# Retention attention feeding a top-1 mixture of experts: the attention stages of a block put in order of TensorE's tile shape

## The chip, the cores and the metric

One core of one Trainium2 chip runs the whole program. The metric is device time in microseconds (us), the median of a few runs. The core has five engines that run side by side and meet at semaphores: TensorE (PE, with its weight loads shown as PEld), VectorE (DVE), ScalarE (ACT), GpSimd (POOL) and SyncE (SP), and 16 DMA engines that move data.

## The reference

For 8 batches, 8 heads, 576 tokens and head size 64, attention is linear with a decay per head; its output goes through one of eight experts per token.

```python
scores = scale * np.matmul(q, k.transpose(0, 1, 3, 2))
gamma = 1.0 - 2.0 ** (-5.0 - np.arange(H))
Dmat = np.where(rel >= 0, gamma[:, None, None] ** rel, 0.0)   # rel = row - column
attn = np.matmul(scores * Dmat, v)                            # [B, H, S, 64]
x = attn.transpose(0, 2, 1, 3).reshape(B * S, H * 64)         # 4608 x 512
logits = x @ w_gate                                           # 8 experts
expert_idx, gate_w = argmax(logits), softmax(logits) at the argmax
for e in range(8):
    out[mask_e] = gate_w[mask_e] * (relu(x[mask_e] @ w1[e]) @ w2[e])   # 512 -> 1024 -> 512
```

## The kernel before

The program has two phases. The first computes the attention, writes its rows in bf16 to a DRAM tensor `x_rows`, and computes the gate's logits and the routing of the first half of the tokens beside it. The second gathers each expert's rows, multiplies them with that expert's weights and scatters the results. Only the first phase is touched by the change.

**Blocks.** A batch is cut into five blocks: c = 0 to 3 have 128 tokens, c = 4 has the remaining 64. There are 40 blocks, and block i is (b, c) = (i // 5, i % 5). The decay is split into a factor on q and one on k, so the masked scores need only a 0/1 mask, and a running state (sum of k times v, kept in the PSUM tile `pss`) carries what earlier blocks contribute. The stages of a block, and the shapes in which they use TensorE's 128 by 128 array:

- `scale_q` and `scale_k` (L241 to L256) run on POOL and multiply q and k by their factors, giving `qq` and `kk`.
- `stage_TQ` and `stage_TK` (L258, L268) transpose `qq` and `kk` on PE (full array, 128 by 128) into a PSUM buffer of the pool `psw`, which has three buffers; ACT copies the result to `qT` (L266) and `kT` (L276). `stage_TQ(b + 1, c)` prepares a quarter of the next batch's q in each of the blocks c = 0 to 3.
- `stage_S` (L279) adds k times v to `pss` (128 by 64) and ACT copies the state to `se` (L293).
- `stage_SC` (L296) computes scores into `pssc` (64 by 64), and DVE multiplies them with the mask into `sc` (L311, L324 for a remainder block).
- `stage_AV` (L331) multiplies scores with values (128 by 64; 64 by 64 in a remainder block) and then the state with q (64 by 64), both into `psx`; DVE copies `psx` to `xT` (L351). In a remainder block ACT first copies half of it (`xo`, L370) and DVE adds the two (`xTr`, L372).
- `stage_R` transposes `xT` back (full array, tile `psr`), ACT casts it to `xr`, and SP stores it to `x_rows`.
- `stage_L1` and `stage_L2`, once a batch, compute the logits (128 by 32, tile `psl`), and transpose them into `lg`.

**Order.** The order on each engine is written out by hand: each engine executes its instructions in the order in which the Python code emits them, and waits at each for its semaphores. The loop `for i, (b, c) in enumerate(blocks)` emits one iteration per block, in a software pipeline: iteration i holds the scores of block i+1, the k transposes of block i+2, the state of block i+1, the transposes back of block i-1, and the value and state products of block i. The scaling runs ahead: iteration i emits `scale_q(b + 1, c)` and `scale_k(i + 3)`.

**Loads.** `load_k(i + 6)`, `load_v(i + 6)` and `load_q(b + 2, ...)` are issued on SP, and the experts' first weights (`load_w`, L224) on POOL, whose DMA casts them to bf16. To pace them, each waits for a mark: a recent instruction named "sc" (the masking), "kT" (the copy of transposed k) or "xT" (the copy of psx), taken as it stands where the load is emitted. One weight load is emitted at the end of iterations 12, 16, 20, 24 and 28, and three at the end of each of the last seven iterations:

```python
early = {12 + 4 * j: [(0, j)] for j in range(5)}
for i in range(NB - 7, NB):
    early[i] = [rest.pop(0) for _ in range(3)]
...
for (e, j), m in zip(early.get(i, ()), ("sc", "kT", "xT")):
    load_w(e, j, 4, wpool, mark.get(m))
```

**Routing.** `route_first` is a Python generator started in block (4, 1), i = 21. It yields an estimated DVE cost after each small instruction, and `steps(rf, budget)` emits instructions until the budget is spent; a `yield None` ends a call at once. Such a break stands ahead of the ranks (PE tile `psrk`, and DVE's `ntot`, `ova`, `rk`, `pos`), ahead of the placing (`pspl`), and ahead of each of the four calls of `gather(e, 0)`, each of which emits two indirect DMAs on POOL.

Of the kernel before, what the change touches and what calls it, by code (L numbers as in the profile page):

```python
# [20 lines left out]
B, H, S, DH = 8, 8, 576, 64  # L21
DM = H * DH
E, F = 8, 1024
NP = H // 2
NCH = 4
# [16 lines left out]
def kernel(  # L42
# [236 lines left out]
    def stage_S(i):  # L279

        if i >= NB:
            return
        b, c = blocks[i]
        kk = kks.pop(i)
        if c == NCH:
            return
        for p in range(NP):
            for j in range(2):
                h = 2 * p + j
                mm(pss[j * DH:(j + 1) * DH, p * DH:(p + 1) * DH], kk[:, h, :], vts[i][:, h, :],  # L290
                   c == 0 and p == 0, c == NCH - 1)
        se = wkp.tile([P, NP, DH], F32, tag="se")
        mark["se"] = nc.scalar.copy(out=se[:, :, :].rearrange("p a d -> p (a d)"), in_=pss[:, 0:NP * DH])  # L293
        sts[(b, c + 1)] = se

    def stage_SC(i):  # L296
        if i >= NB:
            return
        b, c = blocks[i]
        kT = kTs.pop(i)  # L300
        sc = wkp.tile([P, 2, NP, P], F32, tag="sc")
        scs[i] = sc
        if c < NCH:
            qT = qTs[b]
            for p in range(NP):
                for u in range(2):
                    for j in range(2):
                        r = slice(j * DH, (j + 1) * DH)
                        mm(pssc[u * DH:(u + 1) * DH, j, p * P + u * DH:(p + 1) * P], kT[r, p, u * DH:(u + 1) * DH],
                           qT[r, p, c * P + u * DH:(c + 1) * P], True, True)  # L310
            mark["sc"] = nc.vector.tensor_tensor(  # L311
                out=sc[:, :, :, :].rearrange("p j a i -> p j (a i)"), in0=pssc[:, :, :],
                in1=mask[:, :, :].rearrange("p a i -> p (a i)").unsqueeze(1).to_broadcast([P, 2, NP * P]),
                op=ALU.mult)
        else:
            qTs[(b, "r")] = kT
            for p2 in range(2):
                for hf in range(2):
                    p = 2 * hf + p2
                    for j in range(2):  # L320
                        r = slice(j * DH, (j + 1) * DH)
                        mm(pssc[hf * DH:(hf + 1) * DH, j, p2 * P + DH:(p2 + 1) * P], kT[r, p, DH:P], kT[r, p, 0:DH],
                           True, True)
            mark["sc"] = nc.vector.tensor_tensor(  # L324
                out=sc[:, :, 0:2, 0:DH],
                in0=pssc[:, :, :].rearrange("p j (a u i) -> p j a u i", u=2, i=DH)[:, :, 0:2, 1, :],
                in1=tri[:, :].unsqueeze(1).unsqueeze(1).to_broadcast([P, 2, 2, DH]), op=ALU.mult)
# [2 lines left out]

    def stage_AV(i):  # L331
        b, c = blocks[i]
        vt = vts.pop(i)
        sc = scs.pop(i)
        if c < NCH:
            for p in range(NP):
                for j in range(2):
                    o = (j ^ (p % 2)) * DH
                    mm(psx[o:o + DH, j, (p // 2) * P:(p // 2 + 1) * P], vt[:, 2 * p + j, :], sc[:, j, p, :],
                       p < 2, c == 0 and p >= 2)  # L340
            if c > 0:
                se, qT = sts.pop((b, c)), qTs[b]
                for p in range(NP):
                    for j in range(2):
                        o = (j ^ (p % 2)) * DH
                        r = slice(j * DH, (j + 1) * DH)
                        mm(psx[o:o + DH, j, (p // 2) * P:(p // 2 + 1) * P], se[r, p, :], qT[r, p, c * P:(c + 1) * P],
                           False, p >= 2)
            if c == 0:
                xTs[b] = wk1.tile([P, NCH, NP * P], F32, tag="xT", name="xT")  # L350
            mark["xT"] = nc.vector.tensor_copy(  # L351
                out=xTs[b][:, c, :].rearrange("p (w t) -> p w t", w=2), in_=psx[:, :, 0:2 * P])
        else:
            se, qT = sts.pop((b, c)), qTs.pop((b, "r"))
            x = psx[:, :, 256:512].rearrange("p w (a u t) -> p w a u t", a=2, u=2)
            for p2 in range(2):
                for hf in range(2):
                    r = slice(hf * DH, (hf + 1) * DH)
                    for j in range(2):
                        o = (j ^ p2) * DH  # L360
                        mm(x[o:o + DH, hf, p2, hf, :], vt[r, 2 * p2 + j, :], sc[r, j, p2, 0:DH], p2 == 0, False)
            for hf in range(2):
                for p2 in range(2):
                    for j in range(2):
                        r = slice(j * DH, (j + 1) * DH)
                        o = (j ^ p2) * DH
                        mm(x[o:o + DH, j, p2, hf, :], se[r, 2 * hf + p2, :], qT[r, 2 * hf + p2, 0:DH],
                           False, hf == 1 and p2 == 1)
            xo = wk1.tile([P, 256], F32, tag="xo", name="xo")
            nc.scalar.copy(out=xo[:, :], in_=psx[:, 1, 256:512])  # L370
            xTs[(b, "r")] = wk1.tile([P, 256], F32, tag="xTr", name="xTr")
            mark["xT"] = nc.vector.tensor_tensor(out=xTs[(b, "r")][:, :], in0=psx[:, 0, 256:512], in1=xo[:, :],  # L372
                                                 op=ALU.add)
# [70 lines left out]
    def make_routing():  # L444

        nc.gpsimd.memset(lg[:, :, :], 0.0)
        nc.gpsimd.memset(su1[:, :], -1.0)
        nc.gpsimd.affine_select(out=su1[:, :], in_=su1[:, :], pattern=[[-1, P]], base=0, channel_multiplier=1,
                                compare_op=ALU.is_ge, fill=0.0)
        nc.gpsimd.memset(onesb[:, :], 1.0)  # L450
        nc.gpsimd.tensor_copy(out=identb[:, :], in_=ident[:, :])
        nc.gpsimd.iota(iota_r[:, :], pattern=[[1, P]], base=0, channel_multiplier=0,
                       allow_small_or_imprecise_dtypes=True)
        nc.gpsimd.iota(rev[:, :], pattern=[[-1, E]], base=E, channel_multiplier=0,
                       allow_small_or_imprecise_dtypes=True)
        nc.gpsimd.memset(off[:, :], 0.0)
        nc.gpsimd.memset(off[REM:P, :].rearrange("p (b c) -> p b c", c=NCOL)[:, :, NCH:NCOL], 100.0)
        nc.gpsimd.memset(rst[:, :, :], 1.0)
        nc.gpsimd.memset(rst[:, :, 0:1], 0.0)
        nc.gpsimd.iota(hi[:, :], pattern=[[S // 64, B], [2, NCOL]], base=0, channel_multiplier=0,  # L460
                       allow_small_or_imprecise_dtypes=True)
        nc.gpsimd.iota(lo[:, :], pattern=[[1, 1]], base=1, channel_multiplier=1,
                       allow_small_or_imprecise_dtypes=True)
        nc.gpsimd.tensor_copy(out=fld[:, :, 0], in_=hi[:, :])
        nc.gpsimd.tensor_copy(out=fld[:, :, 1], in_=lo[:, :].to_broadcast([P, NT]))
# [170 lines left out]
    def steps(g, budget):  # L636

        while budget > 0:
            try:
                c = next(g)  # L640
            except StopIteration:
                return False
            if c is None:
                break
            budget -= c
        return True
# [38 lines left out]
    rf = None  # L685
    for i, (b, c) in enumerate(blocks):
        if i == 1:
            make_routing()
        if c < NP and b + 1 < B:
            scale_q(b + 1, c)  # L690
        scale_k(i + 3)
        stage_SC(i + 1)
        load_k(i + 6, mark.get("sc"))
        stage_TK(i + 2)
        stage_S(i + 1)
        if c in (1, 3) and b + 2 < B:
            load_q(b + 2, c // 2, mark.get("kT"))
        if rf is not None:
            steps(rf, 0.6)
        if i > 0:  # L700
            stage_R(i - 1)
        if c == 0 and b > 0:
            stage_L1(b - 1)
        stage_AV(i)
        load_v(i + 6, mark.get("xT"))
        if c < NP and b + 1 < B:
            stage_TQ(b + 1, c)
        if c == 0 and b > 0:
            stage_L2(b - 1)
        for (e, j), m in zip(early.get(i, ()), ("sc", "kT", "xT")):  # L710
            load_w(e, j, 4, wpool, mark.get(m))
        if (b, c) == (B // 2, 1):
            rf = route_first()
        if rf is not None:
            steps(rf, 0.8)
    for e, j in rest:
        load_w(e, j, 4, wpool)
    while steps(rf, 1.0):
# [229 lines left out]
```

## Time and profile before

| what | value |
|---|---|
| median of 3 runs | 382.88 us (382.41 to 383.18) |
| the profiled execution's own time | 384.02 us |
| span of its profile | 382.2 us, so 1.8 us lie outside it |
| busy share of PE, PEld, DVE, ACT, POOL | 90%, 64%, 43%, 34%, 52% |
| attention loop, expert phase | until about 207 us, from 212 us |
| one batch of attention in the steady part | 22.57 us |
| DMA, mean | 171 GB/s |

The profile is of one execution. A row of the timeline gives the start and the length in us, the engine, the source line, the operation, the output and input tiles, and the number of instructions merged; in brackets stands the engine's idle time before the row, and what ended it. For PE the array shape that a matmul uses (rows * columns) and the size of the moving operand follow. An fp32 matmul shows as several passes. Matmul ends are modelled, so starts are the better measure. The granted clock is the share of full speed that TensorE was given.

### The profile page before, as it was taken

The page shows a single profiled execution, that of the slowest core. Times are in us where ns is not written, and L with a number is a line of the kernel's source. Part 1 is how long each engine was busy: PE and PEld are TensorE (multiplying, and loading weights), DVE is VectorE, ACT ScalarE, POOL GpSimd, SP SyncE. Part 2 cuts the span into 40 slices and gives each one's busy share as a digit, 9 for nine tenths or more (in the row PEclk, how much of TensorE's full clock was granted, in tenths as well). Part 3 has the DMA queues.
Part 4 walks back from the last instruction along what each step waited for, and adds up shares of the span by engine and source line. Part 5 has one row for each costly group of instructions (what it writes and reads, how often), then busy time and mean ns, then how long its engine had stood idle before and what let it go on. Part 6 is the DMA issues. An engine that isn't in the chain of part 4 may idle for free.

```text
span 382.2 us, 11126 instructions
## 1 busy us (share of the span) xinstructions
PE 342.5 (90%) x4642; PEld 243.2 (64%) x4642; DVE 165.3 (43%) x358; ACT 130.3 (34%) x292; POOL 197.4 (52%) x241
## 2 busy tenths in 40 slices
PE   2599999999999979999994799899999999999960
PEld 1477877778778767877773567555556565656520
DVE  3043343434445786847971695322233232323220
ACT  2224535254353433524331222244322323242410
POOL 4875343453625253587646247867566555554230
PEclk9769999999999999999999699999999999999995
DMA  8958877788888677997999999799789222323120
GB/s 208 250 99 195 204 189 185 168 209 208 206 205 207 162 175 186 180 218 183 196 216 222 207 220 206 199 209 203 178 203 206 93 98 95 103 98 107 63 72 9
DMA packets 113083, 65.34 MB, mean 171 GB/s; under 512 B 83838, under 2 KB 105342, under 8 KB 113024
## 3 DMA queue, kind: packets, MB, share of 16 engines
q0 software_dynamic: 18176, 31.47, 37.3%
q1 hardware_dynamic: 93792, 32.02, 35.1%
q10 hardware_dynamic: 1056, 1.05, 0.9%
q8 instruction: 39, 0.64, 0.7%
q14 instruction: 20, 0.16, 0.2%
HBM read 67.14 MB, written 15.20 MB: 215 GB/s over the span
## 4 chain that ended last, share of the span: by engine, by line
PE 84%; DVE 5%; DMA 4%; POOL 2%; issue 1%; ACT 1%; POOLq 0%; DVEq 0%
PE pm L60 19%; PE py L60 18%; PE psx L60 13%; PE pssc L60 9%; PE psk L63 6%; PE pss L60 5%; PE psr L63 5%; PE psq L63 4%; DMA w1b<-in_moe_w_dram 2%; PE pt L63 2%; PE psl L60 1%; DMA kt<-in_k_dram 1%; DVE xt L757 1%; DVE pay L576 1%; PE pspl L60 1%
## 5 line engine op out<-in xcount | busy, mean ns | idle before, releaser
L773 ACT ACTIVATE ht<-pm 128x384 bf16<-128x384 f32 (+1 forms) x96 | 50.5, 527 | 100.9 <-PE pm L60 100.3
L60 PE MATMUL pm<-xt,w1b 128*128 128x256 bf16 (+1 forms) x512 | 74.5, 305 | 5.4 <-DMA w1b<-in_moe_w_dram 4.9
L788 POOL DMA_INDIRECT out_dram<-ys,tids x40 | 40.9, 1021 | 59.9 <-DVE ys L787 53.2
L60 PE MATMUL py<-w2b,ht 128*128 128x512 bf16 x320 | 71.7, 379 | 0.0
L60 PEld LDWEIGHTS <-w1b 128*128 128x128 bf16 x512 | 51.0, 100 | 28.3 <-DMA w1b<-in_moe_w_dram 5.0
L254 POOL TENSOR_TENSOR kk<-kt,kg 128x512 f32<-128x512 f32 x40 | 41.9, 1056 | 41.0 <-PE pss L60 31.5
L60 PEld LDWEIGHTS <-ht 128*128 128x128 bf16 x320 | 30.7, 98 | 34.1
L311 DVE TENSOR_TENSOR sc<-pssc,mask 128x1024 f32<-128x1024 f32 x32 | 39.1, 1221 | 29.0 <-PE pssc L60 15.3
L787 DVE TENSOR_SCALAR ys<-py,gat 128x512 f32<-128x512 f32 x40 | 30.0, 750 | 47.5 <-PE py L60 46.2
L630 POOL DMA_INDIRECT xg<-x_rows,tidg x40 | 41.1, 1027 | 12.4 <-issue 7.5
L244 POOL TENSOR_TENSOR qq<-qt,qg 128x512 f32<-128x512 f32 x32 | 34.3, 1073 | 19.4 <-PE psq L63 10.3
L351 DVE COPY xT<-psx 128x512 f32<-128x512 f32 x32 | 22.1, 691 | 47.7 <-PE psx L60 47.7
L276 ACT COPY kT<-psk 128x512 f32<-128x512 f32 x40 | 23.4, 586 | 48.8 <-PE psk L63 48.0
L60 PE MATMUL psx<-sc,vt 128*64 128x128 f32 (+1 forms) x640 | 39.2, 270 | 0.0
L757 DVE COPY xt<-pt 128x512 bf16<-128x512 bf16 x40 | 15.5, 420 | 52.6 <-PE pt L63 47.3
L63 PE MATMUL psk<-ident,kk 128*128 128x128 f32 x160 | 27.6, 298 | 11.4 <-POOL kk L254 11.4
L60 PE MATMUL pssc<-qT,kT 64*64 64x64 f32 (+1 forms) x1024 | 37.0, 262 | 0.5 <-ACT se L293 0.5
L60 PEld LDWEIGHTS psx<-sc,vt 128*64 128x64 f32 (+1 forms) x640 | 30.2, 137 | 6.0 <-issue 4.9
L60 PEld LDWEIGHTS pssc<-qT,kT 64*64 64x64 f32 x1024 | 28.7, 137 | 5.7 <-issue 3.1
L232 POOL DMA_DIRECT2D w1b<-in_moe_w_dram x24 | 15.2, 639 | 27.8 <-DVE sc L311 14.9
L266 ACT COPY qT<-psq 128x512 f32<-128x512 f32 x32 | 19.2, 599 | 28.8 <-PE psq L63 28.7
L63 PEld LDWEIGHTS psk<-ident,kk 128*128 128x128 f32 x160 | 17.6, 146 | 17.5 <-POOL kk L254 11.6
(118 smaller groups left out, 350.2 us busy)
## 6 DMA issues: line engine op xcount, KB each, us to landing
kt<-in_k_dram SPq DMA_DIRECT2D x32, 256.0 KB, 4.7
vt<-in_v_dram SPq DMA_DIRECT2D x32, 256.0 KB, 4.3
qt<-in_q_dram SPq DMA_DIRECT2D x14, 512.0 KB, 5.8
x_rows<-xr SPq DMA_DIRECT2D x32, 128.0 KB, 5.4
w1b<-in_moe_w_dram POOLq DMA_DIRECT2D x16, 256.0 KB, 6.9
w2b<-in_moe_w_dram POOLq DMA_DIRECT2D x16, 256.0 KB, 7.6
w1b<-in_moe_w_dram POOLq DMA_DIRECT2D x8, 512.0 KB, 9.6
w2b<-in_moe_w_dram POOLq DMA_DIRECT2D x8, 512.0 KB, 7.6
```

What stands on the lines that cost most here:

```text
L60: nc.tensor.matmul(out=out, lhsT=lhsT, rhs=rhs, start=start, stop=stop, skip_group_check=True)
L63: nc.tensor.transpose(out=out, in_=in_, identity=identity)
L244: nc.gpsimd.tensor_tensor(out=qq[:, :, :].rearrange("p s (h d) -> p h s d", d=DH), in0=qts[b][:, h0:h0 + 2, :, :], in1=qg[:, 0:NCH, h0:h0 ...
L254: nc.gpsimd.tensor_tensor(out=kk[:, :, :], in0=kts.pop(i)[:, :, :], in1=kg[:, blocks[i][1], :].unsqueeze(2).to_broadcast([P, H, DH]), op=A ...
L276: mark["kT"] = nc.scalar.copy(out=kT[:, :, :].rearrange("p a t -> p (a t)"), in_=pst[:, :])
L311: mark["sc"] = nc.vector.tensor_tensor(out=sc[:, :, :, :].rearrange("p j a i -> p j (a i)"), in0=pssc[:, :, :], in1=mask[:, :, :].rearrang ...
L351: mark["xT"] = nc.vector.tensor_copy(out=xTs[b][:, c, :].rearrange("p (w t) -> p w t", w=2), in_=psx[:, :, 0:2 * P])
L630: nc.gpsimd.indirect_dma_start(out=xg[:, :], out_offset=None, in_=x_rows[0:nr, :], in_offset=bass.IndirectOffsetOnAxis(ap=slots[ph][1][:, ...
L757: nc.vector.tensor_copy(out=xt[:, :, j * P:(j + 1) * P], in_=pt[:, :, :])
L773: nc.scalar.activation(out=ht[:, f0:f0 + per, :], in_=pm[:, :, :], func=AF.Relu)
L787: nc.vector.tensor_scalar(out=ys[:, :], in0=py[:, :], scalar1=gat[:, i:i + 1], scalar2=None, op0=ALU.mult)
L788: nc.gpsimd.indirect_dma_start(out=next(outs)[:, :], out_offset=bass.IndirectOffsetOnAxis(ap=tids[:, i:i + 1], axis=0), in_=ys[:, :], in_o ...
```

## The change

The iteration of the block loop is put in another order, so that all stages that use one array shape stand together. The state-times-q part of `stage_AV`, with the copy of `psx`, becomes a stage of its own, `stage_IN`; in a remainder block it also holds the value products. An iteration now runs: k and q transposes, the transposes of the logits (`stage_L2`, one block later than before, at c = 1), the transposes back, the logits, then `stage_S` and `stage_AV`, then `stage_IN` and the scores of block i+1. The two calls of the routing generator become one at the end, with the sum of their budgets. `load_k` is still ahead of the k transposes, so its mark "sc" is now the masking of block i instead of i+1; the weight loads are still at the end of the iteration.

```diff
     def stage_AV(i):
         b, c = blocks[i]
-        vt = vts.pop(i)
-        sc = scs.pop(i)
         if c < NCH:
+            vt = vts.pop(i)
+            sc = scs.pop(i)
             for p in range(NP):
...
+
+    def stage_IN(i):
+
+        b, c = blocks[i]
+        if c < NCH:
             if c > 0:
                 se, qT = sts.pop((b, c)), qTs[b]
...
         else:
+            vt = vts.pop(i)
+            sc = scs.pop(i)
             se, qT = sts.pop((b, c)), qTs.pop((b, "r"))
...
         if c < NP and b + 1 < B:
             scale_q(b + 1, c)
         scale_k(i + 3)
-        stage_SC(i + 1)
         load_k(i + 6, mark.get("sc"))
         stage_TK(i + 2)
-        stage_S(i + 1)
+        if c < NP and b + 1 < B:
+            stage_TQ(b + 1, c)
+        if c == 1 and b > 0:
+            stage_L2(b - 1)
+        if i > 0:
+            stage_R(i - 1)
         if c in (1, 3) and b + 2 < B:
             load_q(b + 2, c // 2, mark.get("kT"))
-        if rf is not None:
-            steps(rf, 0.6)
-        if i > 0:
-            stage_R(i - 1)
         if c == 0 and b > 0:
             stage_L1(b - 1)
+        stage_S(i + 1)
         stage_AV(i)
+        stage_IN(i)
+        stage_SC(i + 1)
         load_v(i + 6, mark.get("xT"))
-        if c < NP and b + 1 < B:
-            stage_TQ(b + 1, c)
-        if c == 0 and b > 0:
-            stage_L2(b - 1)
         for (e, j), m in zip(early.get(i, ()), ("sc", "kT", "xT")):
             load_w(e, j, 4, wpool, mark.get(m))
         if (b, c) == (B // 2, 1):
             rf = route_first()
         if rf is not None:
-            steps(rf, 0.8)
+            steps(rf, 1.4)
```

## The prediction, made before the changed kernel ran

> **What bounds the kernel now.** First the chain of waits on the page: it runs through TensorE (PE) for most of the span.
>
> ```profile
> PE 84%; DVE 5%; DMA 4%; POOL 2%; issue 1%; ACT 1%; POOLq 0%; DVEq 0%
> ```
>
> Then busy time by stretches of one batch of attention (columns: stretch in us, its length, then busy us and instructions of PE, PEld, DVE, ACT, POOL, granted clock, DMA share, GB/s).
>
> ```profile
> 99.61:122.18 22.57, 22.57 (x452) 17.94 (x455) 9.15 (x14) 9.64 (x25) 10.23 (x11) 1.00 0.86 209
> 122.18:147.65 25.47, 23.27 (x456) 18.23 (x458) 19.68 (x41) 9.93 (x26) 10.31 (x10) 1.00 0.71 176
> ```
>
> From 26.86 to 122.18 us PE is busy without a hole and a batch takes 22.57 us each time; every other engine is under half. So what the attention loop is worth is read from PE's start times: the timeline of PE through iteration 12, block (2, 2), into iteration 13 (start, length, engine, line, tiles, array shape).
>
> ```profile
> 76.96 1.09 PE L60 MATMUL pssc<-qT,kT 64*64 64x128 f32 x32
> 77.98 0.66 PE L63 MATMUL psk<-ident,kk 128*128 128x128 f32 x4
> 78.57 0.69 PE L60 MATMUL pss<-vt,kk 128*64 128x64 f32 x16
> 79.18 0.66 PE L63 MATMUL psr<-ident,xT 128*128 128x128 f32 x4
> 79.77 1.09 PE L60 MATMUL psx<-sc,vt 128*64 128x128 f32 x16
> 80.79 0.67 PE L60 MATMUL psx<-qT,se 64*64 64x128 f32 x16
> 81.39 0.66 PE L63 MATMUL psq<-ident,qq 128*128 128x128 f32 x4
> 81.98 0.46 PE L60 MATMUL pssc<-kT 64*64 64x64 f32 x16
> 82.37 0.66 PE L63 MATMUL psk<-ident,kk 128*128 128x128 f32 x4
> 82.86 0.60 PE L63 MATMUL psr<-ident,xT 128*128 128x128 f32 x4
> 83.39 1.09 PE L60 MATMUL psx<-sc,vt 128*64 128x128 f32 x16
> ```
>
> The array shape changes at nearly every row, and a change costs. Four transposes with a change before and after take 0.59 us (77.98 to 78.57); with the change behind them gone 0.49 (82.37 to 82.86), with the one ahead gone 0.53 (82.86 to 83.39). So a change costs 0.10 + 0.06; the step from state products to scores gives 0.11 + 0.04 (0.60 against 0.49 at 193.14 to 193.63, 1.02 against 0.98 there). I take 0.15 us.
>
> **What the reordering saves.** Shape changes per iteration for c = 0 to 4: before 7, 7, 7, 5, 4; after 4, 3, 3, 3, 3. A batch saves 14. Iterations 1 to 33 save 11 + 5 x 14 + 13 = 94, by 0.15: 14.1 us. A full block falls from 5.02 to 4.42 us. Iteration 0 runs at half clock and waits for POOL in both; I put it at nothing.
>
> **What the same move takes away.** Scores of block i+1 now end iteration i, and the q transpose stands second in an iteration instead of last. Look at the weight load that iteration 12 issues (timeline of DVE and POOL):
>
> ```profile
> 78.13 1.23 DVE L311 TENSOR_TENSOR sc<-pssc,mask 128x1024 f32<-128x1024 f32 x1 [0.93 <-PE pssc L60]
> 79.67 0.77 POOL L232 DMA_DIRECT2D w1b<-in_moe_w_dram  x1 [4.30 <-DVE sc L311]
> 80.45 1.08 POOL L244 TENSOR_TENSOR qq<-qt,qg 128x512 f32<-128x512 f32 x1
> ```
>
> POOL had nothing else to do for 4.30 us: the load waits for the mark "sc" of block i+1, and behind it on POOL stands qq of iteration 13. Today qq ends at 81.53 and its transpose comes at 85.01: 3.5 us of cover. Count from s, the start of the scores: qq ends at s + 4.57 (76.96 to 81.53), and in the new order PE reaches its transpose at s + 0.98 (scores) + 0.49 (k transposes) = s + 1.47. PE stands about 3.1 us; with the 0.6 us that the other loads take, 2.95. Everything on PE is queued behind it. Loads go out in iterations 12, 16, 20, 24 and 28; the last has no q transpose behind it (block 29 is a remainder). Four stalls: 12.0 us.
>
> Smaller new waits. (a) Today the scores of block i+1 free one of the two kT buffers just ahead of the k transposes; now they come after them. So at c = 4 ACT's copy to kT (L276) waits for the other buffer's last reader, the remainder's state products, and behind it on ACT stand two xr copies, se and xo. By the pitches of ACT's rows (0.48, then 0.27 each) xo ends 1.73 us after those products, xTr at 2.19, R(i-1) of the next iteration may start at 2.25; PE is there at 1.73. 0.52 us in iterations 5, 10, 15, 20, 30: 2.6 us (25 hides in the stall above). (b) At c = 1 four tiles share three psw buffers and R takes the one that kT's copy reads: free at 1.41 us after the k transposes start (72.96 to 74.30, and a signal), wanted at 1.15: 0.26 in four iterations, 1.0 us. (c) Value products need the masked scores: ready at s + 2.43, wanted at s + 2.97 (2.50 at c = 3): nothing, but only 0.07 to spare at c = 3.
>
> Routing: the batch at 122.18 is 2.90 us longer than its neighbours because a DVE row of 2.91 (ova, L529) held psrk's buffer and the next scores. In the new order the ranks come last in an iteration and only L2 of the next wants that buffer: it waits about 1.0 and psrk takes 0.25. That returns 1.65 us; the slot products (0.82, in the next batch) stay.
>
> At nothing: k, v and q loads on SP and the x_rows stores change places by less than one iteration; loads run six blocks ahead (26 us against 4.7 us to landing), and DMA share rises from 0.75-0.86 to at most 0.95. If that cover went, each late block would cost its lateness. L2 a block later feeds routing only.
>
> Iterations 1 to 33: -14.1 - 1.65 + 12.0 + 2.6 + 1.0 = -0.2 us.
>
> **The last seven blocks.** One routing call an iteration instead of two pushes the eight gathers from iterations 30-31 (POOL 163.69 to 175.9) into iterations 33 to 36, each pair behind three weight loads and ahead of kk. Prices: three w2b loads 2.28 us (179.41), three w1b 1.72, two gathers 2.62 (pitch 1.31), kk 1.05. From T, the start of iteration 34: the masked remainder scores end at T + 0.56, loads to 3.1, gathers to 5.8, kk(37) to 6.85; PE wants it at 3.12. Stall 3.8. Likewise kk(38) at 12.25 against 11.35 (0.95) and kk(39) at 18.85 against 16.76 (2.15). Then, with no q transposes left, masked scores are late for value products at c = 3 by 0.9. The last state products end at T + 28.0; today they end 23.5 us after iteration 34 starts (179.79 to 203.28). Cost 4.5 us.
>
> The leftover routing work (four pay rows at 0.64, twenty one-hot rows at 0.18) falls behind the last block on DVE, two pay rows of it ahead of xTr. About 6 us after xTr: hidden by the last x_rows store, whose landing holds xt until 7.1 us after xTr today (204.17 to 211.26). One microsecond more and it shows. The expert phase is untouched.
>
> **The clock.** Stalls of 3 us are new, and the granted clock reacts to idle PE (same columns as above):
>
> ```profile
> 203.02:206.43 3.41, 1.88 (x63) 1.45 (x53) 0.78 (x2) 1.14 (x5) 2.42 (x5) 1.00 1.16 228
> 206.43:209.85 3.42, 0.79 (x10) 0.61 (x10) 0.28 (x2) 0.00 (x0) 1.63 (x3) 1.00 1.22 219
> 209.85:213.26 3.41, 1.15 (x6) 0.85 (x7) 1.90 (x6) 0.34 (x1) 1.62 (x3) 0.50 1.18 213
> 213.26:216.67 3.41, 3.41 (x18) 2.35 (x17) 3.07 (x12) 1.19 (x2) 1.43 (x2) 0.50 1.13 205
> ```
>
> The clock steps on a grid of 3.41 us. A slice with 1.88 us of PE work kept it, one with 0.79 halved it, and a full slice brought it back. So the limit lies between 1.53 and 2.62 us of idle in one slice; I take 2.1. A 3.0 us stall is caught if a slice ends 2.1 to 4.3 us after it begins. Half clock doubles PE's time (scores 1.97 against 1.02 us): caught after its end (1.3 in 3.41) it loses 1.65, caught before (0.9 in 3.41) two slices, 3.2. Mean 1.5 a stall, 5.9 for four; the 3.8 us stall at the end about 2.0. Bounds over all five: 0 (no gain is possible, the clock being full now) to 16.5.
>
> [...]
>
> **Sum.** -0.2 + 4.5 + 7.9 = +12.2 us. The profiled execution took 384.02 us (span 382.2 and 1.8 around it), 1.1 over the median of the runs, 382.88. So 396.2 on its own scale, 395.1 as a median. Under 0.2% (0.8 us) nothing can be told from no change here.
>
> **Rivals.**
> 1. The same stalls, but no slice is idle enough: +4.3, 387.2 us. For it: 1.43 us holes at 138 us did not move the clock. Against: 0.79 us of work was too little. Chance 0.18.
> 2. Faster: POOL is ahead and qq and kk are there in time. Place: the qq behind each weight load and kk(37) to kk(39). It decides if the mark falls over 3 us earlier than I read it. Then -14.1 - 1.65 + 3.6 before iteration 34 and 21.1 instead of 23.5 us after: -14.5, 368.4 us. Half of it gives 382. Against: POOL's 4.30 us wait names sc L311. Chance 0.08.
> 3. Transfers bound the loop: DMA share is 0.99 from 171 to 203 us, and after that POOL waits for earlier w2b loads to land (3.6 us in four waits). Late weights or stores would add 5 to 10 us to my sum: 400 to 405. Chance 0.08.
> 4. The change does not save: the 0.15 us belongs to waits on semaphores, not to shapes. Then 14.1 more: 409. Against: psr at 82.86 waits for DVE's xT too and follows at 0.49. Chance 0.04.
>
> My own case has 0.62. Range 386 to 404: from no clock loss at all to nearly all slices caught. Faster 0.08, same 0.02, slower 0.90.
>
> **What would show it.** Right: a c = 1 or 2 block of 4.4 us without holes; four holes of about 3 us ahead of psq released by POOL qq, the first after the scores of block 13; half-clock slices after some of them; a hole near 3.8 us ahead of psk released by kk in iteration 35; R released by xTr once a batch. Wrong: no hole ahead of psq after a weight load, or a block still at 5 us, or a clock of 1.00 through all of them.

## The result and the profile after

The changed kernel takes 404.02 us (median of four runs, 399.93 to 405.37) against 382.88 before: a ratio of 1.0535, 95% interval 1.0456 to 1.0615. The profiled execution took 403.17 us (span 401.4), that is 19.15 us more than the 384.02 of the one before. Where executions below are more than 1.5% above the fastest of their kernel (among them one of 672.67 us in experiment 3, two of four in experiment 5, three of four in experiment 8), the medians count them and the ratios do not.

The chain of waits on the page falls apart: TensorE held 84% of it before.

```profile
PE 49%; issue 4%; DVE 3%; POOL 3%; DMA 1%; ACT 1%; SPq 0%; POOLq 0%; DVEq 0%; ACTq 0%
```

What the change says that it does, it does. TensorE's timeline through one full block (c = 2), start to start:

```profile
29.41 0.66 PE L63 MATMUL psk<-ident,kk 128*128 128x128 f32 x4
...
30.86 0.69 PE L60 MATMUL pss<-vt,kk 128*64 128x64 f32 x16
...
32.36 0.67 PE L60 MATMUL psx<-qT,se 64*64 64x128 f32 x16
...
33.83 0.66 PE L63 MATMUL psk<-ident,kk 128*128 128x128 f32 x4
```

Three shapes, three changes, 33.83 - 29.41 = 4.42 us without a hole, where a block took 5.02. What it gives away stands in the view of TensorE's waits (total us, times, longest):

```profile
PE psk L63 <- POOL kk L254: 18.2, 4, 7.2
PE psq L63 <- POOL qq L244: 13.6, 6, 4.0
PE psr L63 <- DVE xTr L379: 4.8, 6, 2.1
```

Of the 18.2, 11.1 lie before iteration 1, as in the kernel before. Of the 13.6, 0.2 lies there too, and 0.9 is a hole in iteration 1. Of the 4.8, 0.95 is the last block's, as before. The rest is new, and the timeline gives each of the large holes (in brackets: idle time ahead of the row, and what ended it):

```profile
81.46 1.12 PE L63 MATMUL psq<-ident,qq 128*128 128x128 f32 x4 [2.94 <-POOL qq L244]
103.19 0.66 PE L63 MATMUL psq<-ident,qq 128*128 128x128 f32 x4 [2.77 <-POOL qq L244]
122.84 1.11 PE L63 MATMUL psq<-ident,qq 128*128 128x128 f32 x4 [2.75 <-POOL qq L244]
144.15 1.11 PE L63 MATMUL psq<-ident,qq 128*128 128x128 f32 x4 [3.98 <-POOL qq L244]
195.92 0.66 PE L63 MATMUL psk<-ident,kk 128*128 128x128 f32 x4 [3.82 <-POOL kk L254]
209.55 0.66 PE L63 MATMUL psk<-ident,kk 128*128 128x128 f32 x4 [3.34 <-POOL kk L254]
```

Four transposes take 0.66 us in some rows and about 1.11 in others: those lie where the granted clock is 0.50 (81.38 to 84.79, 122.33 to 125.75, 142.81 to 149.64). The timeline of DVE and POOL ahead of the first hole shows who is late:

```profile
78.01 1.22 DVE L311 TENSOR_TENSOR sc<-pssc,mask 128x1024 f32<-128x1024 f32 x1 [0.18 <-PE pssc L60]
79.55 0.76 POOL L232 DMA_DIRECT2D w1b<-in_moe_w_dram  x1 [7.24 <-DVE sc L311]
80.33 1.08 POOL L244 TENSOR_TENSOR qq<-qt,qg 128x512 f32<-128x512 f32 x1
```

POOL stood idle for 7.24 us with the load at its head, though the product behind it needed nothing that was missing. The masked scores, now the last work of the iteration, release the load; qq ends at 81.41 and TensorE, idle since 78.52, goes on at 81.46.

In this trace, as in the one before, the changes of the granted clock lie whole multiples of 3.41 us apart: half clock lasts 3.41 us from 81.38, 6.83 from 142.81, and before it lasted 6.83 from 209.85. By slices of that grid (length, then busy us of PE, PEld, DVE, ACT, POOL, granted clock, DMA share, GB/s):

```profile
98.45:101.86 3.41, 1.97 (x52) 1.56 (x48) 1.92 (x2) 0.96 (x2) 0.42 (x1) 1.00 0.77 225
101.86:105.27 3.41, 2.08 (x34) 1.92 (x36) 0.00 (x0) 1.14 (x3) 3.39 (x5) 1.00 0.89 180
118.92:122.33 3.41, 1.17 (x24) 0.76 (x16) 1.53 (x2) 0.59 (x1) 1.20 (x2) 1.00 0.67 152
122.33:125.75 3.42, 2.91 (x21) 2.54 (x22) 0.28 (x2) 1.07 (x3) 2.46 (x3) 0.50 0.71 140
221.32:224.73 3.41, 1.55 (x42) 1.22 (x42) 3.41 (x17) 0.43 (x2) 2.79 (x5) 1.00 1.12 201
224.73:228.14 3.41, 1.51 (x10) 1.18 (x10) 1.46 (x9) 0.00 (x0) 1.26 (x3) 0.50 1.23 213
```

The hole at 100.4 to 103.2 is cut in two by the grid, 1.44 us of idle in one slice and 1.33 in the next, and the clock stays. Of the hole of the same length at 120.1, 2.24 us fall into one slice, and the next runs at half. In the loop the slices from 81.38, 122.33, 142.81 and 146.22 are at half clock.

The expert phase begins (first `pm` row, the first matmul with expert weights) at 229.47 us instead of 212.11: 17.4 of the 19.15 us arise ahead of it.

### The profile page after: what moved, and what is told of

Read it like the earlier page. It is cut to its first block, busy times and chain, and to the rows that moved or that the text cites. A ratio compares the mean times of both kernels' runs of the same rounds, so it can differ in the third digit from the quotient of the medians.

```text
span 401.4 us, 11092 instructions
## 1 busy us (share of the span) xinstructions
PE 338.4 (84%) x4642; PEld 248.8 (62%) x4642; DVE 161.1 (40%) x358; ACT 127.4 (32%) x292; POOL 196.9 (49%) x241
## 3 DMA queue, kind: packets, MB, share of 16 engines
q10 hardware_dynamic: 1056, 1.05, 0.9%
## 4 chain that ended last, share of the span: by engine, by line
PE 49%; issue 4%; DVE 3%; POOL 3%; DMA 1%; ACT 1%; SPq 0%; POOLq 0%; DVEq 0%; ACTq 0%
PE pm L60 18%; PE py L60 17%; PE psx L60 4%; PE pt L63 2%; PE pssc L60 2%; DMA x_rows<-xr 1%; PE psr L63 1%; POOL xg L637 1%; PE pss L60 1%; DVE xt L764 1%; PE psk L63 1%; PE psl L60 1%; PE pspl L60 1%; PE psq L63 1%; POOL kk L254 1%
## 5 line engine op out<-in xcount | busy, mean ns | idle before, releaser
L60 PEld LDWEIGHTS <-w1b 128*128 128x128 bf16 x512 | 51.3, 100 | 25.6 <-DVE xt L764 2.2
L311 DVE TENSOR_TENSOR sc<-pssc,mask 128x1024 f32<-128x1024 f32 x32 | 39.1, 1222 | 19.6 <-issue 13.6
L63 PE MATMUL psk<-ident,kk 128*128 128x128 f32 x160 | 27.1, 293 | 18.2 <-POOL kk L254 18.2
L60 PE MATMUL psx<-sc,vt 128*64 128x128 f32 (+1 forms) x640 | 40.5, 278 | 0.8 <-DVE sc L311 0.8
L60 PE MATMUL pssc<-qT,kT 64*64 64x128 f32 (+1 forms) x1024 | 35.2, 257 | 0.0
L60 PEld LDWEIGHTS psx<-sc,vt 128*64 128x64 f32 (+1 forms) x640 | 32.7, 144 | 3.0 <-DVE sc L311 1.7
L63 PE MATMUL psq<-ident,qq 128*128 128x128 f32 x128 | 22.8, 309 | 13.6 <-POOL qq L244 13.6
L63 PEld LDWEIGHTS psk<-ident,kk 128*128 128x128 f32 x160 | 17.4, 144 | 24.1 <-POOL kk L254 20.0
```

The lines of the kernel that those rows point to most:

```text
L60: nc.tensor.matmul(out=out, lhsT=lhsT, rhs=rhs, start=start, stop=stop, skip_group_check=True)
L63: nc.tensor.transpose(out=out, in_=in_, identity=identity)
L311: mark["sc"] = nc.vector.tensor_tensor(out=sc[:, :, :, :].rearrange("p j a i -> p j (a i)"), in0=pssc[:, :, :], in1=mask[:, :, :].rearrang ...
```

## The experiments

They ran in three series, each on a chip of its own with the kernel before beside them. It took 381.96 us in the first series, 393.65 in the second and 395.94 in the third, so times and ratios are compared within a series; across them I use holes and starts in the traces.

**1. Which part of the move makes the holes: the mark of the load.** First series.

```diff
+        older = mark.get("sc")            # ahead of stage_SC(i + 1)
...
-            load_w(e, j, 4, wpool, mark.get(m))
+            load_w(e, j, 4, wpool, older if i < NB - 7 else mark.get(m))
```

> The five early weight loads (iterations 12 to 28) wait for the masked scores of their own block instead of those of the next; nothing else of the changed kernel moves. My theory (the load holds POOL, and qq behind it is late; the idle time then halves the clock): the four psq holes of 2.75 to 3.98 us (12.4 together) go, and with them the four half-clock slices in the loop; PE worked 3.33, 2.91, 2.07 and 3.42 us in those, half of it lost at most, 5.8. 404.0 - 12.4 - 5.8 = 385.8 us, 383 to 389. If the holes go and the clock was no cost of theirs: 391.6. If qq is late for a reason of its own (its q load, its buffer), or late transfers hold the loop: 402 to 405, with holes ahead of psq still there.

Measured: 383.81 us, ratio 1.0029 (1.0006 to 1.0052). The wait of psq for qq, from the view of its TensorE waits:

```profile
PE psq L63 <- POOL qq L244: 1.1, 2, 0.9
```

That is 0.2 at the start and 0.9 in iteration 1; no slice between 20 and 176 us is below full clock. One argument of five loads takes the ratio from 1.0535 to 1.0029. The spans of the two traces are 401.4 and 382.4 us, 19.0 apart: 12.4 of holes and 6.6 more, of which the four half-clock slices can hold 5.9. Late transfers and a late qq of its own making are out: the same bytes are moved.

**2. Half the delay.** First series.

```diff
-            load_w(e, j, 4, wpool, mark.get(m))
+            load_w(e, j, 4, wpool, mark.get("xT" if i < NB - 7 else m))
```

> The five early loads wait for DVE's xT copy of their own block, which stands a step ahead of the masked scores of the next. It shortens the holes without removing them. My theory: POOL is released some 1.5 us earlier, so three holes shrink from 2.8 to about 1.4 us, and the one of iteration 24, behind xTr, from 4.0 to about 2.9. 6.5 us less idle. On the clock: 1.53 us of idle in a slice of 3.41 kept it before, 2.3 halved it after, so three of the four drops go: about 4 us. 404.0 - 6.5 - 4 = 393.5, 391 to 396. If every hole costs clock in proportion to its length: 404.0 - 6.5 - 3 = 394.5 (not told apart by time; the half-clock slices tell). If a halved clock needs no long hole but any: 397.5.

Measured: 394.99 us, ratio 1.033 (1.029 to 1.037). Two of the four holes in the timeline:

```profile
79.31 0.66 PE L63 MATMUL psq<-ident,qq 128*128 128x128 f32 x4 [1.53 <-POOL qq L244]
...
135.24 1.11 PE L63 MATMUL psq<-ident,qq 128*128 128x128 f32 x4 [2.85 <-POOL qq L244]
```

The four are 1.53, 1.35, 1.17 and 2.85 us, and only the last is followed by a half-clock slice. A later hole of 2.18 us (R for xTr, iteration 30) has one too. So the cost of a hole is not proportional: here the short ones cost their length, the long ones their length and a slice.

**3. POOL's order: products first.** First series.

```diff
+            # end of iteration i, ahead of the weight loads and the gathers
+            scale_q(b1 + 1, c1)           # of iteration i + 1
+            scale_k(i + 4)
```

(The calls at the head of the iteration go; iteration 0 keeps its own.)

> The changed kernel with the qq and kk products of iteration i+1 issued to POOL at the end of iteration i, ahead of its weight loads and routing gathers; nothing else moves. My theory: POOL's order alone makes the holes ahead of psq (12.4 us in iterations 13 to 25) and ahead of psk in the last seven blocks (3.8 + 3.3), and their half-clock slices (5.8 in the loop, about 3 before the expert phase). 404.0 - 12.4 - 7.1 - 8 = 376.5, 373 to 381, below the 382.9 of before. If the holes are made elsewhere (transfers, PE waiting for routing): no lower than 398. If gathers or loads that are issued later now hold the expert phase: 380 to 388, with a hole ahead of pt or pm.

Measured: 373.00 us, ratio 0.9761 (0.9727 to 0.9794), below both kernels. Now the kk holes of the last seven blocks are gone too, as the view of its TensorE waits shows:

```profile
PE psk L63 <- POOL kk L254: 11.4, 2, 7.1
```

The two that remain are those of the start. The load still waits on POOL (4.26 us ahead of the row at 78.17), with nothing behind it that TensorE needs soon. This shows that POOL's order makes the holes at the end as well, the three loads and the two gathers together.

**4. The scores back at the head.** Second series, and again in the third.

```diff
         scale_k(i + 3)
+        stage_SC(i + 1)
...
         stage_IN(i)
-        stage_SC(i + 1)
```

> One part of the change undone: the scores of block i+1 go back to the head of iteration i; the rest of the new order stays. The ring of shapes on TensorE is the same (state product, scores, transposes), so the saving stays. My theory: what cost the time was the place of the scores alone. The weight load's mark comes at the head of the iteration, qq is ready 4.6 us after the scores begin and wanted at 5.9 (4.8 in iteration 25), so the psq holes go; the scores free a kT buffer ahead of the k transposes, so the waits for xTr go (4.4 us with the scores last and no POOL holes); the kk holes of the last seven blocks shrink to 1 us or less, since the mark comes 2.5 us earlier. From the 373.0 with the products issued first: 373.0 - 4.4 + 0 to 1 = 369, 366 to 373. If the saved time needs the scores last (a shape change more per block): 27 x 0.15 = 4 more, 373. If the holes stay: 385 or more.

> The kernel with the scores at the head of the iteration again, now beside the others on one chip. The ratio to the kernel before was 0.965. My theory (all holes ahead of psq gone, the saving of shapes kept): 0.965 again, 0.96 to 0.97, and below the kernel with the products issued first by 2 to 5 us, since it has no wait for xTr in the loop (0.44 x 5 + 1.36 + 0.87 = 4.4 us) but keeps a kk hole of up to 1 us at the end. If the first figure came from the chip that it ran on: 0.975 to 0.98, level with the other.

Measured: 379.77 us, ratio 0.9647 (0.9609 to 0.9685), and 381.00, ratio 0.9626 (0.9579 to 0.9672). The first forecast, 366 to 373, was for the first chip; over the 382.88 of the kernel before it is a ratio of 0.956 to 0.974. In the loop one hole of 0.20 us is left ahead of psq, and R waits for xTr only in the last block; the block keeps 4.42 us, as the timeline shows from scores to scores:

```profile
49.64 1.05 PE L60 MATMUL pssc<-qT,kT 64*64 64x128 f32 x32
...
54.06 0.41 PE L60 MATMUL pssc<-kT 64*64 64x64 f32 x16
```

The order of shapes is a ring, and scores at the head still follow the 64 by 64 state product of the iteration before. So the saving never needed the scores to be last. A batch takes 20.77 us (44.67 to 65.44), against 21.61 with the products first and 22.57 before.

The second half of the second forecast, 2 to 5 us below experiment 3, was not seen. The third series held both:

> The kernel with the qq and kk products issued ahead of the loads, on the same chip as the others: the ratio to the kernel before was 0.976; 0.97 to 0.98 if it does not depend on the chip.

Experiment 3 measured 379.69 there, ratio 0.9519 (0.9446 to 0.9593); its interval and that of the scores-first kernel overlap. In the traces the expert phase starts 2.95 us earlier with the scores first (202.14 against 205.09) and then takes 1.0 longer. Which of the two is the better stays open; both beat the kernel before.

**5. The changed kernel on the third chip.**

> The changed kernel itself, unchanged, on the same chip as the others, so that their differences are taken on one chip. 1.045 to 1.062 of the kernel before if the chip is of no matter; the holes ahead of psq (2.75 to 3.98) and of psk (3.8 and 3.3) the same to 0.1 us, since they are counted in instructions of one core; the half-clock slices may fall elsewhere.

Measured: 412.86 us, ratio 1.0336 (1.0249 to 1.0423). The holes are the same to 0.01 us (2.94, 2.77, 2.75, 3.98; 3.81, 3.34). The half-clock slices fall elsewhere: in this trace, of the longest execution (413.69 us), there are more of them, and the hole at 100 us, spared in the first trace, was caught. The ratio missed the forecast because the kernel before is 13 us slower on this chip, and the changed one only 9 by the median and 6 by the two executions in the ratio (412.72 and 406.76). Why a chip takes 3% longer for the same program is open.

**6. The q transpose last.** Second series.

```diff
-        if c < NP and b + 1 < B:          # behind stage_TK
-            stage_TQ(b + 1, c)
...
         stage_SC(i + 1)
+        if c < NP and b + 1 < B:
+            stage_TQ(b + 1, c)
```

> The changed kernel with the q transpose moved from second in an iteration to last, behind the scores and next to the k transposes of the next iteration: the shape changes stay as few, POOL's order stays, only TensorE asks for qq an iteration later. My theory: qq, ready 4.6 us after the scores begin (about 5.6 in iteration 25), is wanted at 5.4 to 6; the psq holes (12.4) go with their half-clock slices (5.8), the kk holes of the end stay: 384 to 386, 382 to 388 as bounds. If POOL itself is the bound of these iterations: holes of 1 us and more stay, 390 to 396. If the holes are not POOL's: 402 to 405.

Measured: 390.81 us, ratio 0.9941 (0.9906 to 0.9975). The forecast, 382 to 388, was for the first chip; over the 382.88 of the kernel before it is 0.998 to 1.013, so the kernel came out a little faster than forecast. In the trace the psq holes are down to 0.8 us in all, with no half-clock slice between 21 and 180 us, and the expert phase starts at 213.37 us, 16.1 before the changed kernel's 229.47. So it is enough that TensorE asks later; POOL's load did not move. The waits for xTr doubled to 0.87 a batch.

**7. Routing in two calls.** Second series.

```diff
+        if rf is not None:
+            steps(rf, 0.6)                # ahead of stage_R
...
-            steps(rf, 1.4)
+            steps(rf, 0.8)
```

> The changed kernel with the routing work advanced in two calls an iteration (0.6 ahead of the transposes of R, 0.8 at the end) as before, instead of one of 1.4: the eight gathers on POOL leave iterations 33 to 36 and go back to 30 and 31. My theory: of the kk holes (3.82 and 3.34) the gathers make the larger part; the three weight loads alone leave about 1 us (loads end 3.1 us after iteration 34 begins, kk 1.05 later, wanted at 3.12), so 5.5 us go, and one or two half-clock slices with them (3): 404.0 - 5.5 - 3 = 395.5, 392 to 399. The four psq holes stay. If the gathers only move the hole to iterations 31 and 32: 400 to 404, with kk holes there. If the loads alone make the hole: 402 to 405.

Measured: 407.01 us, ratio 1.0304 (1.0226 to 1.0383). The kk holes shrank as expected (TensorE's timeline):

```profile
201.11 0.66 PE L63 MATMUL psk<-ident,kk 128*128 128x128 f32 x4 [1.16 <-POOL kk L254]
...
210.37 0.66 PE L63 MATMUL psk<-ident,kk 128*128 128x128 f32 x4 [0.51 <-POOL kk L254]
```

5.5 us of hole went, and no time with them. The ratio can't tell this, since no run of the changed kernel stands in this series; the traces can: from the scores of block 30 to those of block 39 this kernel takes 51.2 us (166.06 to 217.28) and the changed one 51.3 (166.82 to 218.09). Iterations 30 to 32, with eight gathers on POOL, grew by as much. The rival "the gathers only move the hole" gave the time, though not the place: the largest hole there, 2.43 us at 178.62, is ahead of psr, with no releaser that the profile shows.

**8. The copy xo on DVE,** on top of experiment 3. Second series.

```diff
-            nc.scalar.copy(out=xo[:, :], in_=psx[:, 1, 256:512])
+            nc.vector.tensor_copy(out=xo[:, :], in_=psx[:, 1, 256:512])
```

> The kernel with the qq and kk products issued first (373.0), and the copy xo at the end of a remainder block made by DVE instead of ACT. My theory: xTr is late because xo stands on ACT behind the copy to kT, which waits for the remainder's state products to free a kT buffer. With xo on DVE xTr follows the state products by about 0.8 us and R is never late in the loop: five holes of 0.44, one of 1.36, one of 0.87 go, 4.4 us: 368.6, 367 to 371; the 1.05 at the end is hidden by the x_rows landing. If xTr is late for another reason (DVE's own queue, the routing rows): the two larger holes stay, 371 to 373. If DVE's extra row delays the masked scores: holes ahead of psx.

Measured: 379.68 us, but the four runs lie between 373.66 and 382.39, and the time decides nothing. The trace does: all five holes of 0.44 and the one of 0.87 are gone, so ACT's queue behind the kT copy made them; the one in iteration 30, 1.36 us in experiment 3, is still there with 1.91 and has another cause, as the rival had it for half of the case. DVE's rows show it: four routing rows (rh, L593) that take 4.23 us, from 145.91, stand ahead of xo and xTr (150.05 and 150.50). Why they took so long, when eight such rows take 1.38 at 151.97, is not shown.

**9. The shape change by itself.** Third series, on top of experiment 4.

```diff
-        if i > 0:                         # ahead of stage_S, with L1
-            stage_R(i - 1)
...
         stage_S(i + 1)
+        if i > 0:
+            stage_R(i - 1)                # then L1
         stage_AV(i)
```

> The suspected cost put back alone, with no hole to hide or to add: the kernel with the scores first, and the transposes of R (with L1 behind them at the head of a batch) between the state products and the value products instead of beside the k and q transposes. That adds 2 array shape changes to an iteration with c = 0, 1 or 2, none at c = 3, where there are no state products of the next block, and 1 at c = 4: 7 a batch, 54 in all. At 0.15 us: 8.1 us more than the scores-first kernel, 7 to 10, and a block with c = 1 or 2 longer by 0.30. If shape changes cost nothing and the blocks were shorter for another reason: 0 to 1 us more, and R so late that its waits vanish, perhaps less.

Measured: 389.34 us against 381.00 for experiment 4, 8.3 more; ratio to before 0.9810 (0.9757 to 0.9864). The timeline of its TensorE, one block with c = 2 from scores to scores:

```profile
50.83 1.05 PE L60 MATMUL pssc<-qT,kT 64*64 64x128 f32 x32
...
55.55 0.41 PE L60 MATMUL pssc<-kT 64*64 64x64 f32 x16
```

That is 4.72 us instead of 4.42: 0.15 a change, with the same matmuls. What in a change takes the time, the runs do not tell. The 8.3 is in part luck: a whole batch grew by 0.73 (45.84 to 67.34, against 20.77), not by 7 x 0.15 = 1.05. The c = 1 block grew by only 0.02, since R, now later, no longer waits there for ACT's copy to kT (wait (b) of the prediction). By the scores of block 25 the trace of experiment 4 is 3.7 us ahead (119.79 against 123.52); the iterations with routing, 25, 29 and 30, add 4.9, with holes of 1.12 and 2.32 us ahead of the scores and a half-clock slice. So the price rests on the 4.42 and 4.72, not on the 8.3.

**10. The q transpose alone, in the kernel before.** First series.

```diff
         stage_TK(i + 2)
+        if c < NP and b + 1 < B:
+            stage_TQ(b + 1, c)
...
-        if c < NP and b + 1 < B:          # behind stage_AV
-            stage_TQ(b + 1, c)
```

> The kernel before with one part of the change alone: the q transpose moves beside the k transposes, ahead of the state products; scores stay first. That takes two array shape changes out of each of 27 iterations from 1 on, and opens no hole by my count (qq is ready about 4.6 us after the scores begin, its transpose 6.2). My theory (0.15 us a shape change): 54 x 0.15 = 8.1 less, 382.9 - 8.1 = 374.8 us, 373 to 377, with full blocks of 4.72 us instead of 5.02. If shape changes cost nothing and only the order of waits matters: 382.9. If qq's cover is too short: holes ahead of psq again, 383 to 390.

Measured: 380.37 us, ratio 0.9942 (0.9922 to 0.9962): a gain, but 1.6 us and not 8. Blocks with c = 1 and 2 do take 4.72 us. Two things were missed. At c = 0 nothing is saved (5.50 both times), because the q transpose stood beside those of L2 already; that leaves 0.93 a batch. By the scores of block 24 the trace is 6.6 us ahead (120.54 against 127.13), but 2.3 of that it has by the scores of block 2 (24.50 against 26.79): TensorE came to full clock at 19.69 us instead of 25.53, which no part of the edit explains. Then the routing takes 3.0 back (TensorE's timeline, iteration 25):

```profile
133.44 0.66 PE L63 MATMUL psr<-ident,xTr 128*128 128x128 f32 x2 [3.09 <-DVE rk L531]
```

The DVE row of ova (L529) stands ahead of rk, which reads the buffer that R needs; it took 4.67 us here and 2.91 in the kernel before, and two slices, from 132.33, are at half clock. At the first pm row 3.9 us are left, at the end of the span 2.9 (379.3 against 382.2).

## Why the prediction was right, and where it was short

The forecast was 395.1 us, from 386 to 404; the time is 404.0, at the upper end. The direction and the mechanism are shown: shape changes saved, POOL held by a mark that moved, TensorE stopped behind qq and kk, the clock halved. On the scale of the profiled execution the forecast is 396.2 and the time 403.17, 7.0 short: about 6.1 in iterations 1 to 33, 2.0 in the last seven blocks and 1.9 after them, less 2.9 at the start. There TensorE came to full clock 5.6 us earlier than in the kernel before (19.93 against 25.53), and iteration 1 began at 23.85 instead of 26.79. The prediction put iteration 0 at nothing; that the profiled time is still within the range is due to this, and is luck. By its own steps:

- *Shape changes, 0.15 us each, 94 of them, -14.1.* Right in the price (experiment 9, and 5.02 to 4.42 us a block), nearly in the sum: the scores-first kernel gains 22.57 - 20.77 = 1.80 a batch, with some waits left in it, against 2.1.
- *Four psq stalls of 2.95 (one 3.1), 12.0.* By the brackets 2.94, 2.77, 2.75, 3.98: 12.4. From start to start, as the prediction counted, the q transposes come 3.10, 2.93, 2.92 and 4.14 later than the 0.49 behind the k transposes: 13.1. So the first three were right; the fourth was mis-sized by 1.2, because the wait (a) comes on top of it: its masked scores, of block 25, stand on DVE behind xTr, which is late itself (xTr at 140.57, scores at 140.91, load at 142.43).
- *Wait (a), xTr 0.52 five times, 2.6.* 0.44 by the brackets four times (a block without it, in experiment 8, is 0.5 shorter), hidden in iteration 25 as foreseen, but 2.07 in iteration 30. Its cause in the first four is shown by experiment 8. In iteration 30 it is DVE's queue, as the timelines of DVE and PE show:

```profile
165.64 5.23 DVE L593 TENSOR_SCALAR rh<-iota_r,r 128x128 bf16<-128x128 bf16 x4
170.78 0.41 DVE L379 TENSOR_TENSOR xTr<-psx,xo 128x256 f32<-128x256 f32 x1
171.25 0.44 PE L63 MATMUL psr<-ident,xTr 128*128 128x128 f32 x2 [2.07 <-DVE xTr L379]
```

  ACT's xo had ended at 168.82; four routing rows held DVE for 5.23 us, which the text had at 0.18 each.
- *Wait (b), 0.26 at c = 1, 1.0.* Right: at c = 1 R starts 1.38 us behind the k transposes (46.09 to 47.47), just after ACT's copy to kT (46.83 to 47.42); the text had 1.41. But the iteration takes 4.93, 0.51 over the 4.42, for L2's own time moved there too. And there is a wait at c = 4 that the text did not have: R starts 0.74 us behind the k transposes instead of 0.49 (37.14 to 37.88), because DVE's copy to xT ends only at 37.74 and no q transposes stand between. An iteration with c = 4 takes 3.41, and 3.14 with the scores first.
- *Routing, -1.65.* Not visible in the changed kernel between the holes. In experiment 3 iterations 22 to 34, which hold most of the routing, take 56.6 us, before 61.1: 4.5 less, of which 2.8 is what such iterations gain without routing, so -1.7.
- *To the start of iteration 34:* forecast -0.2 and 5.9 of clock, +5.7 from iteration 1 on. Measured +11.8 (23.85 to 188.62 against 26.79 to 179.79). This is the step that failed, by terms that the sum lacked or had too small. Iteration by iteration, against the forecast for each: iteration 1, put at no wait, 1.1 (a hole of 0.91 ahead of psq, for qq); iterations 6, 11, 16 and 31, with c = 1, 1.0; those with c = 4, 0.7; iteration 10, 0.8, with a break of 0.52 in the logits for which the profile names no releaser; iterations 30 and 32, 1.6, most of it xTr; the stalls with clock and routing 0.9.
- *Last seven blocks, 4.5 + 2.0.* From iteration 34 to the first pm row the kernel takes 40.85 us, before 32.32: +8.5. kk(37) 3.82 as forecast (3.8); kk(38) nothing instead of 0.95; kk(39) 3.34 instead of 2.15; masked scores late by 0.77 (0.9). That TensorE's half clock after the first hole gave POOL time for kk(38) is argued only. The clock was caught twice, not once (half-clock slices from 197.43 and 211.08).
- *Clock, 5.9 for the four stalls.* Three of the four were caught, four slices in all, with 3.33, 2.91, 2.07 and 3.42 us of work: half of that, 5.9, is the most that they can have cost. Had the clock held through all four, the forecast would have been 387; half clock followed from 81.38, 122.33 and 142.81, behind slices with 0.56, 1.17 and 0.78 us of work, so the trace decides against that.
- *The expert phase untouched.* It takes 1.9 us longer. 0.5 is the clock: it is at half until 5.5 us after the first pm row (234.97), instead of 4.6 (216.67), and TensorE keeps a lag of 0.5 to its last products. The text did not carry the clock over the end of the attention. The other 1.4 arise behind TensorE: from its last row to the end of the span 14.5 us (from 386.92) instead of 13.1 (from 369.09). What makes them is open.

The rivals: no clock drop (387) is refuted by the half-clock slices. POOL ahead (368) is refuted, and is just what experiment 3 brings about by hand, at 373. "Transfers bound the loop" (400 to 405) names the measured time but not its cause: with the same bytes and one mark changed the time is 383.8. "It does not save" is refuted by the 4.42.

## What to carry to other kernels

When a step is moved, look for every semaphore it raises and ask what in-order queue has an instruction waiting for it: here a weight load, of no urgency itself, held the engine that feeds the bottleneck (POOL stood idle for 7.24 us with the load at its head). Put urgent work ahead of waiting work on such a queue (381.96 us before, 373.00 in experiment 3 of the same series), or keep the releasing step early; here a saving worth 9 us had turned into a loss of 21. And price a hole on TensorE by where it lies: in these traces it cost its length, and, where the holes in one slice of 3.41 us left TensorE too little work there (less than 1.4 us always, from 1.4 to 2.0 sometimes), a slice or more at half clock as well.

## What was not expected of the hardware

- The clock fell after slices with more work than I took, and with the same work not always. In the first 300 us of all fourteen traces its changes lie whole multiples of 3.41 us apart. The changed kernel's hole of 2.77 us, cut in two, was followed by full clock (slices with 1.97 and 2.08 us of work); in experiment 5 the same hole lay in one slice, from 99.99, with 0.64 us of work, and half clock followed. Between 26 and 300 us each slice at full clock with less than 1.4 us of TensorE work (its ends are modelled) was followed by one at half clock, and none with more than 2.0 was; in between both occur, from 1.40 (spared, experiment 9, from 245.61) to 2.0 (caught, experiment 7, from 185.66). The changed kernel's hole at 192.1 has both, in two slices with the same work:

```profile
190.60:194.01 3.41, 1.50 (x65) 1.25 (x64) 0.93 (x2) 1.69 (x5) 2.80 (x5) 1.00 0.84 126
194.01:197.43 3.42, 1.51 (x34) 1.35 (x38) 0.62 (x1) 0.77 (x3) 3.39 (x5) 1.00 1.15 243
197.43:200.84 3.41, 3.41 (x56) 3.00 (x44) 0.36 (x1) 0.53 (x2) 2.79 (x4) 0.50 0.98 152
```

  The prediction's limit, 2.1 us of idle, is 1.3 of work: the slices with 1.51 and 1.55 that were caught lie above it.
- In some traces everything but POOL stops together. Experiment 4 on the third chip, one stretch (columns as above):

```profile
186.75:188.35 1.60, 0.00 (x0) 0.00 (x0) 0.00 (x0) 0.00 (x0) 1.34 (x2) 1.00 1.07 168
```

  POOL issues gathers and weight loads then. The rows of DVE and ACT that follow it name only "remote" as what they waited for. They begin at 188.40 and 188.46, 0.4 us after the second gather's row ends; the same kernel in the second series (187.67, 0.36 after) and experiment 9 (196.27, 0.35 after) go on in the same way. The first series has no such hole in experiment 3. What it is, I leave open.
